# Moving the product of the two gates from GpSimd to VectorE in a gated-attention and multiplicative-FFN kernel

## The chip, the cores and the metric

The kernel runs on one core of one Trainium2 chip. The core has TensorE for matrix products (in the profile PE, its weight loads PEld), VectorE (DVE), ScalarE (ACT), GpSimd (POOL) and SyncE (SP), which here only issues transfers. Each engine takes its instructions strictly in order; across engines they wait for each other by semaphores. The metric is the time of one execution on the device in microseconds (us), the median of several runs.

## The reference

Two blocks follow each other. The first is a recurrent attention with a decaying state, for 4 batches and 8 heads over 768 steps with head size 48:

```python
for t in range(S):
    state = alpha[:, :, t, :, None] * state + np.einsum('bhd,bhe->bhde', k[:, :, t], v[:, :, t])
    y[:, :, t] = np.einsum('bhd,bhde->bhe', q[:, :, t], state)
```

Its output, reshaped to 3072 tokens of 384 values, is the input x of the second block:

```python
a = x @ w1          # 384 -> 1024
b = x @ w2          # 384 -> 1024
h = a * b @ w3      # 1024 -> 1024
return (h @ w_out).astype(np.float32)   # 1024 -> 384
```

The change touches the elementwise product a * b. The four weight matrices come in 64-bit floating point.

## The kernel before

Tokens are handled in 24 chunks of 128, and for the second block in 8 groups of 384 tokens. The feature dimension of 1024 is cut into 8 tiles of 128, so there are 64 tiles of a * b, each 128 features by 384 tokens in 32-bit floats.

A product of full precision is made from three products of reduced precision (`exact`, lines 352 to 363). Each operand is split into a high part, a low part and a mixed part. `exact` does 2n products into one PSUM bank (L358), ScalarE copies that bank scaled into a tile t (L360), TensorE does n products into a second bank (L362), and VectorE combines bank and t (L363). For a gate n is 3.

`gate(g, f)` (L365) does this twice, for w1 and w2, and so gets two tiles r in SBUF. The tiles r and t come from a pool with two buffers each. Then the two r are multiplied into a tile ab (L374, three buffers), and SyncE stores ab to DRAM (L381); in the program the store of a tile is written behind the product of the next one (`store_ab`).

The program has three parts. In the first, the loop over the 24 chunks does the recurrence (matrix products of 48 and 128 columns, masks on VectorE at L308, decays on VectorE at L247, a small product of the state's decay on GpSimd at L294 to L296), converts w1 and w2 from 64 to 32 bits and splits them, and does the first gates in between, half a gate at a time. x goes through DRAM: it is stored by chunk (L336), loaded by group (L341) and split by ScalarE (L347) and VectorE (L348, L349).

In the second part the remaining gates run one after the other. Between them lies the conversion of w_out and w3: `to_fp32` loads a piece of raw 64-bit words (L171, three buffers), takes it apart on ScalarE (L179, L184) and VectorE (L180, L183), and puts it together on VectorE (L186, L187, L189). L187 is the last to read a raw buffer. When a row block of w3 is converted, `fold` transposes it (L401, L403), multiplies it by w_out (L407) and splits the result on ScalarE (L410) and VectorE (L411, L412): w3 and w_out become a single matrix of 1024 by 384.

In the third part the stored ab tiles are loaded (L418), split (L425 to L427) and multiplied by that matrix, again by `exact`, and the output is stored (L434).

The program is written against a planner. It records the instructions in program order with their dependencies, and then orders those of each engine by program priority and by its own estimates of when each can start and how long it takes. So an engine's order on the chip is not always that of the text; L186, L187 and L189 of one piece, for instance, are written together and often stand apart, with L363 of a gate between. The semaphores are placed by the same planner. Raw loads, loads of x and stores of ab all go through SyncE's one queue.

Of the kernel before, what the change touches and what calls it, by code (L numbers as in the profile page):

```python
# [48 lines left out]
def kernel(  # L49
# [12 lines left out]
    nc = tc.nc  # L62
# [289 lines left out]
    def exact(to, w, x, scale):  # L352

        p1, p2 = (bank()[:, 0:to.shape[1]] for _ in range(2))
        n = len(w[0])
        for part in range(2):
            for i in range(n):
                nc.tensor.matmul(p1, w[part][i], x[part][i], start=(part == i == 0), stop=(part == 1 and i == n - 1))  # L358
        t = gw.tile(list(to.shape), FP32, tag="t", name="t")
        nc.scalar.activation(t, p1, AF.Copy, scale=(1.0 + 1.0 / P) * scale)  # L360
        for i in range(n):
            nc.tensor.matmul(p2, w[2][i], x[2][i], start=(i == 0), stop=(i == n - 1))  # L362
        nc.vector.scalar_tensor_tensor(to, p2, -scale, t, op0=ALU.mult, op1=ALU.add)  # L363

    def gate(g, f):  # L365
        r = []
        x = [[st["x3", g][:, part, kk, :] for kk in range(KM)] for part in range(3)]
        for w, scale in zip(w12, (1.0, P * P)):
            r.append(gw.tile([C, TG], FP32, tag="r", name="r"))
            exact(r[-1], [[w[:, part, kk, ds(f * C, C)] for kk in range(KM)] for part in range(3)], x, scale)  # L370
            if len(r) == 1:
                yield
        ab = abp.tile([C, TG], FP32, tag="ab", name="ab")
        nc.gpsimd.tensor_mul(ab, *r)  # L374
        store_ab()
        st["ab"] = g, f, ab

    def store_ab():
        if "ab" in st:
            g, f, ab = st.pop("ab")  # L380
            nc.sync.dma_start(out=abd[g][:, f, :], in_=ab)  # L381
# [92 lines left out]
    for n in range(N):  # L474
        load_a(n + 5)
        load(n + AHEAD)
        scores(n)
        convert(1)
        run(1)
        store_x(n - 1)  # L480
        advance(n)
        outer(n)
        transposed(n + 1)
        decayed(n + 2)
        logs(n + 4)
        convert(2 if n in (0, 1, 2, 3, 4, 5) else 1)
        run(1)
        decays(n + 3)
        load_ends(n + 2)
        convert(1)  # L490
        attend(n)
        if n + 2 in begin:
            load_x(begin[n + 2])
        if n in begin:
            split_x(begin[n], 0)
            fill.extend(gate(begin[n], f) for f in range(FH))
# [20 lines left out]
    for k, (g, tiles) in enumerate(visits):  # L517
        order.append((max(len(todo) - 4, order[-1][0] + 1 if order else 0), len(todo), g, 1 - k % 2))
        todo += [gate(g, f) for f in tiles]
# [59 lines left out]
```

## Time and profile before

| | |
|---|---|
| median of 3 runs | 527.57 us (527.34 to 528.01) |
| profiled execution, its own time | 531.2 us |
| span of the profiled execution | 529.4 us |
| mean granted TensorE clock | 0.973 of full speed |
| GpSimd at L374 | 64 instructions, 78.1 us busy |
| VectorE at L363 for gates | 128 instructions, 69.0 us busy |

The profile records one execution. "Busy" is the time in which an engine had an instruction under way. A row of the timeline gives the start in us from the beginning of the span, the duration, the engine, the source line, the operation, the tile written and the tile read, the number of instructions put together in the row (x), and in brackets the idle time of that engine before it and what ended it. Rows put together overlap a little at their ends. A row of the waits gives who waited, for whom, the total in us, how often, and the longest. SPq is SyncE's queue of transfers.

### The profile page before, as it was taken

Reading aid. Unit: us, or ns where it says so; the run is one execution under the profiler, and the core shown is the slowest. Engines: PE = TensorE matmul, PEld = TensorE weight load, DVE = VectorE, ACT = ScalarE, POOL = GpSimd, SP = SyncE. Lnnn points to the kernel's source line nnn. Section 1 sums busy time; section 2 is a strip of 40 time slices with the busy share of each in tenths; the row PEclk is TensorE's granted clock in tenths of the full one; section 3 lists DMA queues with packets and bytes.
Section 4 is the critical chain, followed back from the end, with each engine's and each line's share of the span. In section 5 each row is a group of like instructions: output and inputs, shape, how many; then the busy total and the mean of one; then the engine's idle time right before and its main releaser. Section 6 shows DMA issues by size and latency. Waiting matters only on the chain. (4 is left out here: it accounts for less than half of the span.)

```text
span 529.4 us, 9440 instructions
## 1 busy us (share of the span) xinstructions
PE 493.5 (93%) x3568; PEld 438.7 (83%) x3568; DVE 366.0 (69%) x546; ACT 245.1 (46%) x443; POOL 96.3 (18%) x105
## 2 busy tenths in 40 slices
PE   3889599999999999998898499999999999999997
PEld 1667478888888888998786388888899999999996
DVE  2699987975545645999999578854365347676771
ACT  3567656564545544545445244433353233343330
POOL 1032012121201121223221422221224310000000
PEclk9979989999999999999899879999999999999999
DMA  9999999889986632555555432220184126555621
GB/s 161 241 187 191 226 213 206 207 170 204 207 201 121 195 117 82 163 173 170 183 176 184 139 110 90 70 91 30 47 226 147 67 79 184 166 165 169 180 79 45
DMA packets 167805, 80.25 MB, mean 152 GB/s; under 512 B 112696, under 2 KB 163152, under 8 KB 167760
## 3 DMA queue, kind: packets, MB, share of 16 engines
q1 hardware_dynamic: 158240, 79.58, 58.3%
q10 hardware_dynamic: 9520, 0.07, 1.1%
q8 instruction: 28, 0.46, 0.4%
q14 instruction: 17, 0.14, 0.1%
HBM read 57.58 MB, written 22.06 MB: 150 GB/s over the span
## 5 line engine op out<-in xcount | busy, mean ns | idle before, releaser
L358 PE MATMUL bank<-x,w 128*128 128x384 f32 x768 | 164.8, 349 | 8.6 <-ACT x L347 5.3
L358 PEld LDWEIGHTS bank<-x,w 128*128 128x128 f32 x768 | 135.5, 191 | 15.0 <-ACT x L347 5.4
L360 ACT ACTIVATE t<-bank 128x384 f32<-128x384 f32 x152 | 73.6, 490 | 122.4 <-PE bank L358 104.1
L374 POOL TENSOR_TENSOR ab<-r 128x384 f32<-128x384 f32 x64 | 78.1, 1221 | 220.7 <-DVE r L363 201.7
L363 DVE SCALAR_TENSOR_TENSOR r<-bank,t 128x384 f32<-128x384 f32 x128 | 69.0, 551 | 62.7 <-ACT t L360 35.9
L362 PE MATMUL bank<-x,w 128*128 128x384 f32 x384 | 90.0, 343 | 9.9 <-ACT t L360 8.5
L362 PEld LDWEIGHTS bank<-x,w 128*128 128x128 f32 x384 | 69.6, 192 | 12.1 <-ACT t L360 9.1
L358 PE MATMUL bank<-w3o,ab 128*128 128x384 f32 x384 | 70.4, 334 | 0.0
L358 PEld LDWEIGHTS bank<-w3o,ab 128*128 128x128 f32 x384 | 66.9, 188 | 0.0
L407 PE MATMUL bank<-wo,w3T 128*128 128x384 f32 x128 | 43.6, 494 | 0.0
L179 ACT ACTIVATE rest<-raw 128x512 f32<-128x512 uint32 (+1 forms) x36 | 23.4, 649 | 33.3 <-DMA raw<-in_moe_w_dram 23.9
L184 ACT ACTIVATE power<-power,rebias 128x512 uint32<-128x512 uint32 (+1 forms) x36 | 25.0, 700 | 27.7 <-DVE power L183 27.5
L407 PEld LDWEIGHTS bank<-wo,w3T 128*128 128x128 f32 x128 | 24.8, 194 | 15.4 <-issue 0.9
L308 DVE TENSOR_TENSOR ms<-bank,keep 128x512 int32<-128x512 int32 x48 | 31.2, 682 | 9.1 <-PE bank L305 8.9
L426 DVE TENSOR_TENSOR ab<-abl,ab 128x1024 fp32r<-128x1024 f32 x24 | 30.1, 1253 | 10.4 <-ACT ab L425 10.4
L362 PE MATMUL bank<-w3o,ab 128*128 128x384 f32 x192 | 37.2, 334 | 0.0
L247 DVE TENSOR_TENSOR qk<-kq,e 128x768 f32<-128x768 f32 x24 | 23.0, 958 | 17.7 <-ACT e L239 16.7
L267 ACT COPY qkT<-bank 128x512 f32<-128x512 f32 x48 | 26.1, 588 | 19.2 <-PE bank L266 19.1
L425 ACT ACTIVATE ab<-abl 128x1024 fp32r<-128x1024 f32 x24 | 25.5, 1062 | 19.2 <-PE bank L362 18.8
L362 PEld LDWEIGHTS bank<-w3o,ab 128*128 128x128 f32 x192 | 33.6, 188 | 0.0
L363 DVE SCALAR_TENSOR_TENSOR o<-bank,t 128x384 f32<-128x384 f32 x24 | 13.4, 558 | 26.8 <-issue 15.2
L427 DVE SCALAR_TENSOR_TENSOR ab<-ab,abl 128x1024 fp32r<-128x1024 f32 x24 | 29.3, 1219 | 0.0
(59 smaller groups left out, 568.1 us busy)
## 6 DMA issues: line engine op xcount, KB each, us to landing
raw<-in_moe_w_dram SPq DMA_DIRECT2D x28, 512.0 KB, 5.3
abd<-ab SPq DMA_DIRECT2D x64, 192.0 KB, 2.2
abl<-abd SPq DMA_DIRECT2D x24, 512.0 KB, 5.4
xT<-xd SPq DMA_DIRECT2D x14, 576.0 KB, 3.9
ac<-in_alpha_dram SPq DMA_DIRECT2D x24, 192.0 KB, 4.4
kq<-in_k_dram SPq DMA_DIRECT2D x24, 192.0 KB, 5.3
kq<-in_q_dram SPq DMA_DIRECT2D x24, 192.0 KB, 4.1
v<-in_v_dram SPq DMA_DIRECT2D x24, 192.0 KB, 4.9
```

The costliest lines, as they stand in the source:

```text
L184: nc.scalar.activation(power, power, AF.Relu, scale=2.0 ** 23, bias=rebias)
L267: nc.scalar.copy(qkT[:, i], tp.rearrange("p (j c) -> p j c", j=NP))
L308: nc.vector.tensor_tensor(ms[:, i].bitcast(I32), sc[i].bitcast(I32), keep_bc, op=ALU.bitwise_and)
L358: nc.tensor.matmul(p1, w[part][i], x[part][i], start=(part == i == 0), stop=(part == 1 and i == n - 1))
L360: nc.scalar.activation(t, p1, AF.Copy, scale=(1.0 + 1.0 / P) * scale)
L362: nc.tensor.matmul(p2, w[2][i], x[2][i], start=(i == 0), stop=(i == n - 1))
L363: nc.vector.scalar_tensor_tensor(to, p2, -scale, t, op0=ALU.mult, op1=ALU.add)
L374: nc.gpsimd.tensor_mul(ab, *r)
L407: nc.tensor.matmul(po, w3T[:, j, :], wo[:, j, :], start=(j == 0), stop=(j == KF - 1))
L425: nc.scalar.activation(t[:, 0], ab, AF.Copy, scale=1.0 - 2.0 ** -13)
L426: nc.vector.tensor_sub(t[:, 1], ab, t[:, 0].bitcast(FP32))
L427: nc.vector.scalar_tensor_tensor(t[:, 2], t[:, 0].bitcast(FP32), 1.0 + 1.0 / P, ab, op0=ALU.mult, op1=ALU.subtract)
```

## The change

The instruction that multiplies the two gate tiles is issued to VectorE instead of GpSimd. Operands, buffers, the store and all loops stay as they were.

```diff
--- before.py
+++ after.py
@@ -371,7 +371,7 @@
             if len(r) == 1:
                 yield
         ab = abp.tile([C, TG], FP32, tag="ab", name="ab")
-        nc.gpsimd.tensor_mul(ab, *r)
+        nc.vector.tensor_mul(ab, *r)
         store_ab()
         st["ab"] = g, f, ab
```

## The prediction

> **What bounds the kernel now.** I read the page's engine shares first, then busy time by stretch, then who made TensorE wait, then the timeline around its longest gap.
>
> ```profile
> span 529.4 us, 9440 instructions
> PE 493.5 (93%) x3568; PEld 438.7 (83%) x3568; DVE 366.0 (69%) x546; ACT 245.1 (46%) x443; POOL 96.3 (18%) x105
> ```
>
> TensorE (PE) is the engine of the span, so a gain can only come out of its idle time or its slow clock. The stretches (columns: length, busy us and count per engine, clock, DMA share, GB/s) say where that lies:
>
> ```profile
> 229.00:262.00 33.00, 29.26 (x154) 27.62 (x153) 33.00 (x50) 16.05 (x30) 11.48 (x10) 0.95 0.61 187
> 262.00:297.00 35.00, 32.93 (x167) 27.61 (x166) 33.98 (x55) 17.74 (x32) 11.51 (x7) 1.00 0.44 142
> 297.00:314.00 17.00, 9.99 (x29) 7.49 (x29) 9.95 (x17) 6.31 (x12) 2.65 (x2) 0.70 0.54 172
> 314.00:426.00 112.00, 112.00 (x593) 101.08 (x592) 63.52 (x96) 43.45 (x80) 29.12 (x25) 1.00 0.31 96
> ```
>
> From 229 to 297 VectorE (DVE) is busy 66.98 of 68 us and TensorE is not: there VectorE sets the pace, with the weight conversion, the splits and the gates all on it. From 297 to 314 nearly everything stands still; from 314 on TensorE has no gap. What TensorE waited for between 229 and 300:
>
> ```profile
> PE bank L358 <- DVE r L363: 2.8, 3, 1.8
> PE bank L362 <- DVE w3o L412: 1.0, 1, 1.0
> PE bank L362 <- ACT t L360: 0.9, 1, 0.9
> PE bank L358 <- ACT t L360: 0.5, 1, 0.5
> ```
>
> That is 5.2 us of short waits. The long gap comes after them, in the timeline:
>
> ```profile
> 290.77 0.54 DVE L363 SCALAR_TENSOR_TENSOR r<-bank,t 128x384 f32<-128x384 f32 x1
> 291.24 0.67 DVE L187 SCALAR_TENSOR_TENSOR power<-raw,power 128x512 uint32<-128x512 uint32 x1
> 291.45 5.41 POOL L374 TENSOR_TENSOR ab<-r 128x384 f32<-128x384 f32 x1 [3.82 <-DVE r L363]
> ...
> 296.89 0.33 SPq L381 DMA_DIRECT2D abd<-ab  x1
> 297.38 0.33 SPq L171 DMA_DIRECT2D raw<-in_moe_w_dram  x1
> ...
> 302.54 0.66 ACT L179 ACTIVATE rest<-raw 128x512 f32<-128x512 uint32 x1 [9.71 <-DMA raw<-in_moe_w_dram]
> ...
> 304.01 1.33 PE L362 MATMUL bank<-x,w 128*128 128x384 f32 x3 [7.53 <-ACT t L360]
> 305.14 2.12 PE L358 MATMUL bank<-x,w 128*128 128x384 f32 x6
> ...
> 308.02 6.31 PE L407 MATMUL bank<-wo,w3T 128*128 128x384 f32 x16
> ```
>
> One product took 5.41 us on GpSimd. Its store (L381) stood at the head of SP's queue until 296.89, the raw weight load (L171) stood behind the store, and ScalarE stood at L179 for that load with L360, whose result TensorE needed, behind it. TensorE idled 7.53 us and then ran slowly.
>
> Why a product that mostly takes 1.0 us took 5.41, and what products do to VectorE, is seen where the two engines meet:
>
> ```profile
> L374 POOL TENSOR_TENSOR ab<-r x64: 992/1019/5412, 75.3 to 426.5; 128x384 f32<-128x384 f32 x64
> 253.88 1.33 POOL L374 TENSOR_TENSOR ab<-r 128x384 f32<-128x384 f32 x1 [2.82 <-DVE r L363]
> 254.26 2.16 DVE L348 TENSOR_TENSOR x<-xT,x 128x1152 fp32r<-128x1152 f32 x1
> ```
>
> L348 starts under the running product and ends 2.16 us later; it lasts until shortly after GpSimd has finished. Groups of VectorE instructions between 215 and 297 (count, then busy us and mean ns) show the same on other lines; the two last rows give the undisturbed duration (the last: minimum/median/maximum, smaller and larger shape):
>
> ```profile
> L186 DVE SCALAR_TENSOR_TENSOR mant<-mant,rest 128x512 f32<-128x512 uint32 x11 | 9.7, 885 | 0.1
> L187 DVE SCALAR_TENSOR_TENSOR power<-raw,power 128x384 uint32<-128x384 uint32 x5 | 5.2, 1040 | 0.0
> L183 DVE TENSOR_SCALAR power<-raw 128x512 uint32<-128x512 uint32 x10 | 6.6, 658 | 0.0
> L180 DVE TENSOR_SCALAR mant<-raw 128x512 uint32<-128x512 uint32 x11 | 6.2, 563 | 0.0
> L183 DVE TENSOR_SCALAR power<-raw 128x384 uint32<-128x384 uint32 x4 | 3.0, 761 | 0.0
> L180 DVE TENSOR_SCALAR mant<-raw 128x384 uint32<-128x384 uint32 x4 | 3.0, 757 | 0.0
> L187 DVE SCALAR_TENSOR_TENSOR power<-raw,power 128x512 uint32<-128x512 uint32 x10 | 6.8, 678 | 0.0
> L180 DVE TENSOR_SCALAR mant<-raw x36: 345/416/1237, 18.8 to 337.7; 128x512 uint32<-128x512 uint32 x28, 128x384 uint32<-128x384 uint32 x8
> ```
>
> A disturbed L180 takes 1.24 where 0.42 is normal: 0.82 us lost. The excess of the six rows is 11 x 0.207 + 5 x 0.495 + 10 x 0.242 + 11 x 0.147 + 4 x 0.416 + 4 x 0.412 = 12.1 us, that is 15 meetings (the plain 128x384 two-input operation takes 0.545, shown below). L348 above is one more; I count 18 meetings for the stretch's 19 products, 14.5 us. So the two engines exclude each other: VectorE loses 0.8 us to nearly every product, and where VectorE runs such operations back to back from 291.24 on, GpSimd is the one that stands.
>
> **The change, part by part.** *Removed:* 64 products on GpSimd, with what they cost VectorE and SP. *Added:* 64 products on VectorE, on the same 128x384 f32 operands in SBUF. Nothing else changes in the text of the kernel; the store stays on SP and waits for VectorE instead. The price:
>
> ```profile
> L189 DVE TENSOR_TENSOR wo<-mant,power x8: 541/545/562, 211.1 to 243.6; 128x384 f32<-128x384 f32 x8
> 257.61 1.01 DVE L363 SCALAR_TENSOR_TENSOR r<-bank,t 128x384 f32<-128x384 f32 x2
> 96.16 0.68 DVE L187 SCALAR_TENSOR_TENSOR power<-raw,power 128x512 uint32<-128x512 uint32 x1
> 96.87 0.69 DVE L189 TENSOR_TENSOR mant<-mant,power 128x512 f32<-128x512 f32 x1
> ```
>
> L189 is the same operation on the same shape: 0.545 us. Two 0.55 us operations in a row take 1.01, so a following operation starts 0.46 after the first. But L189, which reads what L187 just made, starts only 0.71 after it, past its whole 0.68. The product reads the second r straight after it is written, so it costs 0.46 plus the lost overlap of 0.09 and 0.03 of start: 0.58 us. The lower bound, 0.46, holds if the order puts something between. Added between 215 and 297: 19 x 0.58 = 11.0 us, with no cover, since VectorE is full there; the other 45 (26 us) fall where it has idle time, 63.52 busy of 112 after 314 for instance; were that cover gone they would cost their 26 us. The product adds no wait on r (same engine, in order). It must still find its ab buffer stored; there are three, so the store two tiles back must hang for that to bind, and I put it at nothing. SP's queue keeps its order of store and loads, and what is moved past on GpSimd is only the small products of the recurrent state, which then meet no gate product.
>
> Step 1, VectorE's pace, 215 to 297: 14.5 - 11.0 = 3.5 us less VectorE work, which TensorE's short waits (5.2 us) can give back. Bounds 0 (the waits sit elsewhere) and 5.2.
>
> In the Trainium skill, "VectorE: DVE Perf Modes", section "The DRAIN you can't avoid", the next operation does not start until the pipe has emptied; by it every product would cost 0.62, not 0.58, and step 1 would be 2.8. The 1.01 us row contradicts it for independent operations, so I stay at 0.58.
>
> Step 2, the late load: the second r ends at 291.31, the product at about 291.9. L187, which frees the raw buffer, moves behind it and ends near 292.5. The store goes out at 291.9, the load at 292.5 instead of 297.38: 4.9 us earlier, and with the same landing time ScalarE and TensorE resume 4.9 us earlier. The gap shrinks from 7.53 to 2.6. Bounds: 0 (something else holds the load) and 7.5.
>
> Step 3, the clock. Undisturbed rows against those after gaps:
>
> ```profile
> 243.26 1.31 PE L358 MATMUL bank<-x,w 128*128 128x384 f32 x6 [1.76 <-DVE r L363]
> 258.21 1.82 PE L358 MATMUL bank<-x,w 128*128 128x384 f32 x6 [0.87 <-DVE r L363]
> 264.06 0.68 PE L362 MATMUL bank<-x,w 128*128 128x384 f32 x3
> 268.59 5.32 PE L407 MATMUL bank<-wo,w3T 128*128 128x384 f32 x16
> ```
>
> After the 7.53 us gap 1.33, 2.12 and 6.31 stand for 0.68, 1.31 and 5.32: 2.45 us. The clock of 0.95 over 33 us costs 1.65 more. A gap of 1.76 brought no slow row, shorter ones near 258 did, so whether 2.6 us does is open: I take half of both, 2.0 us, bounds 0 and 4.1.
>
> The Trainium skill ("TensorE: Matmul & The Clock Gate", "What's actually happening") has the clock halved after an idle window of about 3.4 us; by it a 2.6 us gap would keep full clock and step 3 would be nearer 4. The 258.21 row, slow after gaps under 1 us, does not follow it.
>
> Sum: 3.5 + 4.9 + 2.0 = 10.4. The profiled execution took 531.2 (1.8 us around its span), 3.6 above the median of 527.57; 531.2 - 10.4 = 520.8, and the same off the median gives 517.2. All idle and clock loss gone would be 5.2 + 7.5 + 4.1 = 16.8: 510.8.
>
> **Rivals.** *Half of it.* The load is early but another wait takes its place, or VectorE stays as full because the order shifts: only step 1, or half of step 2. Gain 2.5 to 6, about 523. For it: ScalarE and SP run in order, and with both engines near full in 229 to 297 small delays add up.
>
> *Slower: the product stuck in VectorE's queue.*
>
> ```profile
> DVE w3o L411 <- ACT w3o L410: 19.6, 6, 6.2
> SPq L381 <- POOL ab L374: 165.1, 52, 8.8
> ```
>
> On GpSimd a product waits for its r alone. On VectorE it waits for all ahead of it, and L411 has stood up to 6.2 us. If the planner, which orders each engine's instructions by its own costs, puts products behind such waits, the store, the load behind it, L179 and TensorE follow as at 291 to 304: 7.5 + 2.45 = 10 us a place. One place eats the gain, a second decides: 517.2 + 20 = 537. Against it: the product is ready the moment r is, and most VectorE waits lie after 314, where the loads have slack.
>
> *No change.* The 5.41 us product belongs to the profiled execution alone and VectorE's relief is used up by other waits: 527.6. Against it: the 0.8 us losses are everywhere in the stretch.
>
> **How the numbers follow.** Likeliest (its own range 512 to 521.5): 0.60. Half: 0.22. Slower: 0.10. No change: 0.08. A measurement tells 0.2% (1.05 us) from nothing, so faster (below 526.5) is 0.82, same 0.08, slower 0.10. The range runs from just under the bound of 510.8 to 526.5, leaving out the last two cases.
>
> **What would show it.** Right: no instruction of GpSimd at L374; L374 on VectorE at about 0.55; L180, L183 and L186 at 0.42, 0.42 and 0.68 with maxima near these; no store waiting 5 us on SP before 300; the gap before L362 near 304 at 3 us or less; the clock of that stretch above 0.9. Wrong: VectorE's busy time between 215 and 297 not falling, a new TensorE gap over 3 us behind ScalarE's L179, or products standing long after their r.

## The result and the profile after

The changed kernel takes 514.56 us (median; 512.42 to 515.54) against 527.79 before, 13.2 us less between the medians; the ratio over all runs is 0.9726 with a 95% interval of 0.9664 to 0.9787, that is 2.7% faster. The forecast was 517.2, its range 510.0 to 526.5. The executions of the kernel before spread over 525 to 534 us, some near 527 and most near 532, which the last experiment looks into. Its profiled execution, at 531.2, is one of the long ones, so the two traces lie further apart (15.6 us of span) than the medians.

The engine shares of the page after:

```profile
span 513.8 us, 9439 instructions
PE 488.9 (95%) x3568; PEld 436.8 (85%) x3568; DVE 373.0 (73%) x610; ACT 246.0 (48%) x443; POOL 17.9 (3%) x41
```

64 products on VectorE raised its busy time by only 7.0 us, because what they cost is nearly paid by what it no longer loses. The stretches of the trace after, columns as before:

```profile
229.00:262.00 33.00, 31.61 (x184) 31.34 (x184) 32.42 (x65) 19.36 (x36) 0.00 (x0) 1.00 0.66 196
262.00:297.00 35.00, 35.00 (x172) 29.16 (x172) 33.09 (x63) 19.77 (x35) 0.00 (x0) 1.00 0.55 173
297.00:314.00 17.00, 17.00 (x85) 14.24 (x84) 16.89 (x32) 8.98 (x17) 0.00 (x0) 1.00 0.61 185
314.00:410.00 96.00, 96.00 (x512) 87.32 (x511) 61.85 (x105) 37.78 (x70) 0.00 (x0) 1.00 0.32 99
```

VectorE is nearly as full as before, but TensorE does not wait for it, and the clock is 1.00 throughout. All that TensorE waited for from the end of the attention part to its last fold is in one row of its waits:

```profile
PE bank L401 <- DVE w L189: 1.4, 1, 1.4
```

Since the stages shift, a stretch bounded by instructions compares better than one bounded by times: from TensorE's last L323 (the end of the attention part) to its last L407 (the last fold). What follows, the rest of the gates and the third part, takes 140.4 us in both traces, up to TensorE's last instruction. The two halves of the stretch, which meet at TensorE's first L401, the start of the first fold, are summed here (length, then busy us of each engine), first before, then after:

```profile
sum 174.10, PE 161.28 PEld 140.90 DVE 136.26 ACT 77.68 POOL 43.47; mean PE 80.64 PEld 70.45 DVE 68.13 ACT 38.84 POOL 21.74
```

```profile
sum 156.36, PE 154.97 PEld 137.42 DVE 131.95 ACT 78.80 POOL 0.00; mean PE 77.49 PEld 68.71 DVE 65.97 ACT 39.40 POOL 0.00
```

The stretch is 17.7 us shorter. VectorE's work in it fell by 4.3 us although it took on the products; its idle time, 174.10 - 136.26 = 37.8 before, is 24.4 after. The attention part gave 1.9 us of the gain back (it ended at 213.02 instead of 211.07 us), which lies within its spread: 211.1 to 215.8 in all traces of this study that keep the first part's start.

Single instructions on VectorE (minimum/median/maximum): L183 before, then three lines after, the product and two of the lines that had met products:

```profile
L183 DVE TENSOR_SCALAR power<-raw x36: 344/415/1240, 19.1 to 338.5; 128x512 uint32<-128x512 uint32 x28, 128x384 uint32<-128x384 uint32 x8
```

```profile
L374 DVE TENSOR_TENSOR ab<-r x64: 546/557/559, 78.2 to 410.6; 128x384 f32<-128x384 f32 x64
L183 DVE TENSOR_SCALAR power<-raw x36: 344/419/430, 19.4 to 322.8; 128x512 uint32<-128x512 uint32 x28, 128x384 uint32<-128x384 uint32 x8
L186 DVE SCALAR_TENSOR_TENSOR mant<-mant,rest x36: 546/683/994, 21.4 to 324.7; 128x512 f32<-128x512 uint32 x28, 128x384 f32<-128x384 uint32 x8
```

The maximum of L183 fell from 1240 to 430 ns. The 994 of L186 lies in the attention part, where the small products of the state are still on GpSimd.

### The profile page after: what moved, and what is told of

The parts are those of the page before. It is cut to its first block, busy times and chain, and to the rows that moved or that the text cites. A ratio compares the mean times of both kernels' runs of the same rounds, so it can differ in the third digit from the quotient of the medians.

```text
span 513.8 us, 9439 instructions
## 1 busy us (share of the span) xinstructions
PE 488.9 (95%) x3568; PEld 436.8 (85%) x3568; DVE 373.0 (73%) x610; ACT 246.0 (48%) x443; POOL 17.9 (3%) x41
## 4 chain that ended last, share of the span: by engine, by line
PE 91%; DVE 3%; DMA 3%; ACT 1%; issue 1%; SPq 0%; ACTq 0%; DVEq 0%
PE bank L358 40%; PE bank L362 20%; PE bank L407 8%; PE bank L305 4%; PE bank L266 4%; PE bank L323 4%; PE bank L319 4%; PE bank L235 3%; PE bank L277 2%; PE bank L401 1%; DMA xT<-xd 1%; DMA ac<-in_alpha_dram 1%; DMA dec<-ends 1%; DVE power L187 1%; DVE ms L308 0%
## 5 line engine op out<-in xcount | busy, mean ns | idle before, releaser
L358 PE MATMUL bank<-x,w 128*128 128x384 f32 x768 | 162.2, 345 | 6.2 <-ACT x L347 6.1
L358 PEld LDWEIGHTS bank<-x,w 128*128 128x128 f32 x768 | 133.8, 189 | 11.1 <-ACT x L347 6.3
L360 ACT ACTIVATE t<-bank 128x384 f32<-128x384 f32 x152 | 74.1, 491 | 129.0 <-PE bank L358 115.5
L363 DVE SCALAR_TENSOR_TENSOR r<-bank,t 128x384 f32<-128x384 f32 x128 | 69.7, 553 | 53.2 <-ACT t L360 44.1
L362 PE MATMUL bank<-x,w 128*128 128x384 f32 x384 | 88.0, 336 | 0.0
L362 PEld LDWEIGHTS bank<-x,w 128*128 128x128 f32 x384 | 68.7, 189 | 0.8 <-PE bank L358 0.5
L407 PE MATMUL bank<-wo,w3T 128*128 128x384 f32 x128 | 42.6, 486 | 0.0
L407 PEld LDWEIGHTS bank<-wo,w3T 128*128 128x128 f32 x128 | 24.1, 190 | 14.9
L374 DVE TENSOR_TENSOR ab<-r 128x384 f32<-128x384 f32 x64 | 35.5, 554 | 1.1
L363 DVE SCALAR_TENSOR_TENSOR o<-bank,t 128x384 f32<-128x384 f32 x24 | 13.4, 558 | 26.6 <-issue 15.6
L247 DVE TENSOR_TENSOR qk<-kq,e 128x768 f32<-128x768 f32 x24 | 22.9, 953 | 13.5 <-ACT e L239 13.2
L179 ACT ACTIVATE rest<-raw 128x512 f32<-128x512 uint32 (+1 forms) x36 | 23.4, 651 | 15.9 <-DMA raw<-in_moe_w_dram 9.1
```

The costliest lines, as they stand in the source:

```text
L374: nc.vector.tensor_mul(ab, *r)
L407: nc.tensor.matmul(po, w3T[:, j, :], wo[:, j, :], start=(j == 0), stop=(j == KF - 1))
```

## The experiments

The theory to test had two parts: VectorE and GpSimd exclude each other, which slows VectorE by 0.8 us a product (step 1), and a starved product holds SP's queue and with it a raw load (steps 2 and 3). The rivals: the planner's new order alone, or the product's shorter way to SP. Ratios are to the kernel before as it ran in the same batch; its median was 531.53 us up to the run with one product moved and 530.69 us after that.

**Exclusion put back in part, order kept.** GpSimd multiplies each finished product by itself into an unused tile. In its trace the order of instructions on TensorE, VectorE and SyncE is that of the changed kernel.

```diff
-        ab = abp.tile([C, TG], FP32, tag="ab", name="ab")
+        ab, twin = (abp.tile([C, TG], FP32, tag=x, name=x, bufs=n) for x, n in (("ab", 3), ("twin", 1)))
...
         nc.vector.tensor_mul(ab, *r)
+        nc.gpsimd.tensor_mul(twin, ab, ab)
```

> The product stays on VectorE; GpSimd multiplies each finished product tile by itself into a tile that nobody reads. The outputs are computed as before. The order on TensorE, VectorE, ScalarE and SyncE is that of the changed kernel. Theory (the two engines exclude each other, about 0.8 us of VectorE for each meeting): VectorE pays 0.46 to 0.58 for its own product and 0.8 for the twin, 12 to 15 us more in a stretch that is full, so the gain is lost: 525 to 540 us, L180, L183, L186 and L187 again with maxima of 1.2 to 1.5 us. Rival (the gain comes from the new order, or from the product reaching SyncE's queue sooner): nothing waits for the twin, so 512 to 516 us.

524.18 us, ratio 0.9909 (0.9869 to 0.9949): 9.6 us of the 13.2 are lost again, just short of the range expected. The sum of the stretch in this run:

```profile
sum 163.68, PE 158.11 PEld 138.68 DVE 140.66 ACT 78.13 POOL 38.13; mean PE 79.05 PEld 69.34 DVE 70.33 ACT 39.06 POOL 19.07
```

Two groups of its instructions, by line:

```profile
L186 DVE SCALAR_TENSOR_TENSOR mant<-mant,rest x36: 546/680/1305, 21.6 to 334.8; 128x512 f32<-128x512 uint32 x28, 128x384 f32<-128x384 uint32 x8
L374 POOL TENSOR_TENSOR twin<-ab x64: 825/942/1939, 79.9 to 421.5; 128x384 f32<-128x384 f32 x64
```

The maxima of L186 and L187 come back as expected (1.31 and 1.32 us); those of L180 and L183 reach only 1.05. Nobody reads the twin, so its cost is exclusion: 7.3 us in the stretch (163.68 - 156.36), with VectorE 8.7 us busier. A rival without exclusion has no way to explain this. But the twins put back only a part of the exclusion, because they meet other instructions than the products did (L349, which no product had lengthened, has a median of 1.98 us here instead of 1.35). Measured against the median of the same line and shape in the changed kernel, VectorE's instructions in the stretch last 9.2 us too long here; in the kernel before it was 21.0 us, 0.6 us for each of its 34 products there. The stretch is still 10.4 us shorter than before, although VectorE is 4.4 us busier than it was then: the amount of VectorE's work is not all that counts.

**Only one part of the products moved.**

```diff
-        nc.vector.tensor_mul(ab, *r)
+        (nc.vector if "late" in st else nc.gpsimd).tensor_mul(ab, *r)
...
     part1.close()
+    st["late"] = True
```

> Only the products traced after the first part go to VectorE; those of the first part, where the attention chunks run, stay on GpSimd. Theory: TensorE had no idle time to give back before 215 us, so all of the gain is here: 512 to 517 us. Rival (the first part's products delay the weight conversion or the loads that the second part then lacks): only part of the gain, 518 to 525 us.

514.29 us, 0.971 (0.9659 to 0.9762): the whole gain, as the theory expected. The reverse, with the two engines exchanged in that line:

> The reverse: only the products of the first part go to VectorE. Theory: 526 to 529 us, as before, with one product of 4 us or more on GpSimd and a TensorE gap behind it still there near 290 to 304. Rival (the first part matters): 518 to 524 us.

531.05 us, 0.9966 (0.9917 to 1.0015): nothing that can be told from no change. Both expected ranges were missed; the theory's 526 to 529 lay around the 527.57 of the first runs, while the kernel before had a median of 531.53 in this batch. The starved product is still there, as the group of the products left on GpSimd shows:

```profile
L374 POOL TENSOR_TENSOR ab<-r x47: 992/1070/5411, 216.6 to 427.4; 128x384 f32<-128x384 f32 x47
```

So the 17 products of the attention part are worth nothing either way: from 75 us, where the first product starts, to 211 us TensorE has no gap over 0.4 us to give back.

**One product moved.**

```diff
-        nc.gpsimd.tensor_mul(ab, *r)
+        st["count"] = st.get("count", 0) + 1
+        (nc.vector if st["count"] == 36 else nc.gpsimd).tensor_mul(ab, *r)
```

> Only the 36th product, the one that took 5.41 us on GpSimd, goes to VectorE; the other 63 stay. Theory of the late load (steps 2 and 3 of the prediction, 7.5 us of gap and 2.45 us of slow clock): most of the gain comes from this one product, 517 to 521 us. Rival (VectorE's pace is what counts, and with the other 63 on GpSimd the next product is starved or the next load late instead): 525 to 528 us.

526.75 us, 0.9931 (0.9899 to 0.9963): 4.8 us below the median of the kernel before in this batch (531.53). The expectation of 517 to 521 failed; the time is in the rival's range. The sum of the stretch in its trace:

```profile
sum 167.00, PE 159.38 PEld 138.39 DVE 135.48 ACT 77.10 POOL 38.99; mean PE 79.69 PEld 69.20 DVE 67.74 ACT 38.55 POOL 19.50
```

Its timeline of TensorE at the end of what had been the long gap (start, length, instruction, and in brackets the wait before it):

```profile
301.03 0.79 PE L362 MATMUL bank<-x,w 128*128 128x384 f32 x3 [1.56 <-ACT t L360]
301.70 1.31 PE L358 MATMUL bank<-x,w 128*128 128x384 f32 x6
```

The long gap is 1.56 instead of 7.53 us and nothing runs slowly behind it. The stretch is 7.1 us shorter than in the profiled execution of the kernel before; 10.6 us remain to the changed kernel.

**The store taken out of SP's queue.** The product stays on GpSimd, which issues its store too.

```diff
-            nc.sync.dma_start(out=abd[g][:, f, :], in_=ab)
+            nc.gpsimd.dma_start(out=abd[g][:, f, :], in_=ab)
```

> The product stays on GpSimd, and GpSimd issues its store too, so that SyncE's queue and the raw loads in it no longer wait for a product. Theory of the late load as in the prediction (a store that waits for its product holds the raw load): the long gap near 296 to 304 falls to 3 us or less, the exclusion stays, 523 to 528 us. Rival (SyncE's queue waiting for GpSimd products is most of the difference between the two kernels): 514 to 518 us.

526.33 us, 0.9925 (0.9889 to 0.996), as the theory expected. The sum of the stretch in its trace:

```profile
sum 165.94, PE 158.44 PEld 136.88 DVE 135.86 ACT 77.12 POOL 65.87; mean PE 79.22 PEld 68.44 DVE 67.93 ACT 38.56 POOL 32.94
```

Its timeline, the starved product on GpSimd and the end of the gap that had been the long one on TensorE:

```profile
293.30 5.46 POOL L374 TENSOR_TENSOR ab<-r 128x384 f32<-128x384 f32 x1 [2.90 <-DVE r L363]
299.51 0.79 PE L362 MATMUL bank<-x,w 128*128 128x384 f32 x3 [1.18 <-ACT t L360]
```

The product is starved as before, 5.46 us, behind the same VectorE lines, and TensorE hardly notices: 1.18 us. The planner also moved some other VectorE and ScalarE instructions here, but together with the single-product run, which moves hardly any, this shows the path of the long gap: product, store, raw load. It also shows that SP's queue is not the rest of the gain.

**The product twice on VectorE.**

```diff
-        ab = abp.tile([C, TG], FP32, tag="ab", name="ab")
+        ab, twin = (abp.tile([C, TG], FP32, tag=x, name=x, bufs=n) for x, n in (("ab", 3), ("twin", 1)))
         nc.vector.tensor_mul(ab, *r)
+        nc.vector.tensor_mul(twin, *r)
```

> As changed, and VectorE multiplies the same pair a second time into a tile that nobody reads. Nothing else is left out. Theory (VectorE still sets the pace from 215 to 314 us, where it was busy 96 of 99 us after the change): about 25 extra products of 0.47 to 0.58 us there without cover, 12 to 14 us: 522 to 528 us, with TensorE idle again in that stretch. Rival (TensorE sets the pace, VectorE's fullness is work done ahead of need): 514 to 517 us.

524.36 us, 0.987 (0.9795 to 0.9945), inside the theory's range. The sum of the stretch in this run:

```profile
sum 164.22, PE 157.98 PEld 139.77 DVE 147.11 ACT 78.82 POOL 0.00; mean PE 78.99 PEld 69.89 DVE 73.56 ACT 39.41 POOL 0.00
```

TensorE's longest gap in it, from the timeline:

```profile
267.90 1.09 PE L401 MATMUL bank<-ident,w 128*128 128x128 f32 x4 [4.01 <-DVE w L189]
```

VectorE is 15.2 us busier and the stretch 7.9 us longer: about half of what is added shows. In the twin run above 8.7 us more gave 7.3. The planner moved other VectorE instructions in this run too, so the size is less sure than in the twin run. Both say that after the change VectorE stands close behind TensorE and has little to spare.

**A GpSimd instruction that only writes.** One of the two r tiles is filled with zeros after each product, before it is written anew.

```diff
         nc.vector.tensor_mul(ab, *r)
+        nc.gpsimd.memset(r[0], 0.0)
```

> As changed, and GpSimd fills one of the two gate tiles with zeros behind each product; the tile is not read again before it is written anew. So GpSimd has one instruction per product again, on the same size, which only writes SBUF. Theory (the exclusion is with GpSimd instructions that read SBUF; on two-input VectorE instructions a fill has no effect): 514 to 518 us, L186, L187 and L348 at their undisturbed durations, at most L180 and L183 longer. Rival (any GpSimd instruction on SBUF stops VectorE): as with the twin, 521 to 526 us.

515.27 us, 0.97 (0.9637 to 0.9762), as the changed kernel. The group of the fills in this run:

```profile
L374 POOL MEMSET r<- x64: 413/418/1587, 78.5 to 411.5; 128x384 f32 x64
```

One place of its timeline where a fill meets the conversion:

```profile
313.37 0.41 DVE L180 TENSOR_SCALAR mant<-raw 128x512 uint32<-128x512 uint32 x1
313.56 1.59 POOL L374 MEMSET r<- 128x384 f32 x1 [4.12 <-DVE ab L374]
...
314.38 0.42 DVE L183 TENSOR_SCALAR power<-raw 128x512 uint32<-128x512 uint32 x1
314.71 0.68 DVE L186 SCALAR_TENSOR_TENSOR mant<-mant,rest 128x512 f32<-128x512 uint32 x1
315.31 0.68 DVE L187 SCALAR_TENSOR_TENSOR power<-raw,power 128x512 uint32<-128x512 uint32 x1
```

The fill takes 0.42 us alone and 1.59 here: it stood while four L180 and L183 ran in a row and was done 0.44 us after L186 began, during L186, which kept its 0.68. So a fill excludes the one-input L180 and L183 and not the two-input L186, while a product, which reads SBUF, had excluded both. In the Trainium skill, "SBUF — State Buffer", section "Who interferes with whom", a VectorE instruction with two inputs in SBUF contends with a GpSimd instruction that reads SBUF and not with one that only writes, and one in the fast two-port mode contends with either. These rows agree with the first; they agree with the second if L180 and L183 run in that mode, which no trace here shows.

**The first gates one chunk later.**

```diff
-    begin = {6 + 4 * g: g for g in range(5)}
+    begin = {7 + 4 * g: g for g in range(5)}
```

> As changed, with the first gates begun one chunk later (7 + 4g instead of 6 + 4g). After the change nearly all of TensorE's idle time lies before the first gate, 6.1 us of it waiting for the first x tile at 62 to 68 us. Theory: chunk work fills that wait, 509 to 513 us. Rival (the chunk work there waits for its own input loads, and the gates put off come back later): 514 to 518 us.

521.95 us, 0.983 (0.9767 to 0.9893): slower than the changed kernel, and outside both expected ranges. The timeline of TensorE in this run, where the chunk work now stands ahead of the first gate:

```profile
65.64 1.65 PE L235 MATMUL bank<-la,after 128*128 128x384 f32 x2 [2.80 <-ACT la L227]
...
76.39 1.33 PE L358 MATMUL bank<-x,w 128*128 128x384 f32 x3 [3.74 <-ACT x L347]
```

The wait of 6.1 us became two, 2.80 for the chunk's input and 3.74 for the x tile, and the first gate began 8 us later. The attention part ended as in the changed kernel (212.84 us); the stretch up to the last fold is 1.8 us longer, and what follows it 3.1 us. So the gates put off came back later, as the rival said, and cost more than it expected.

**The kernel before, unchanged, in four more executions.**

> The kernel before, unchanged, profiled once more. Its times lie in two groups, 525 to 529 us and 531 to 534 us. If the late load comes in some executions only: an execution of 530 us or more has a product of 5 us and a TensorE gap of over 6 us behind it, one of 525 to 529 us has neither a gap over 3 us after 215 us. If the late load is always there: the gap is in it whatever its time.

> The same kernel as the look before, once more, with the same expectation: the long gap goes with the time of 530 us or more, or it is always there.

> The kernel before once more, to meet an execution of 525 to 529 us: if the long gap is not always there, such an execution lacks it; one of 530 us or more has it again.

> As the look before it: an execution of 525 to 529 us without the long gap, or one of 530 us or more with it.

Times: 533.6, 531.43, 527.89 and 534.24 us. The first, second and fourth have a product of 5.41 to 5.42 us on GpSimd and a TensorE gap of 7.14, 7.25 and 7.54 us behind it. The third has neither in that size: its longest gap after 215 us is 2.98 us, just under the 3 us expected of a short execution. The third's sum of the stretch:

```profile
sum 169.04, PE 159.62 PEld 138.42 DVE 136.37 ACT 77.05 POOL 40.65; mean PE 79.81 PEld 69.21 DVE 68.19 ACT 38.52 POOL 20.32
```

Its timeline at the same place as in the prediction, and the gap:

```profile
293.11 0.69 DVE L187 SCALAR_TENSOR_TENSOR power<-raw,power 128x512 uint32<-128x512 uint32 x1
293.32 1.34 POOL L374 TENSOR_TENSOR ab<-r 128x384 f32<-128x384 f32 x1 [3.92 <-DVE r L363]
293.71 1.51 DVE L186 SCALAR_TENSOR_TENSOR mant<-mant,rest 128x512 f32<-128x512 uint32 x1
...
301.42 0.88 PE L362 MATMUL bank<-x,w 128*128 128x384 f32 x3 [2.98 <-ACT t L360]
302.10 2.28 PE L358 MATMUL bank<-x,w 128*128 128x384 f32 x6
```

Here GpSimd got through and L186 stood, 1.51 for 0.68 us. In the long executions L186 went first and the product stood. So the starved product comes in some executions and not in others, and the five executions put its price in the stretch at 4 to 5 us (173.0 to 174.1 against 169.0). The single-product run is another 2.0 us shorter in the stretch. It is 3.5 us shorter behind the first fold (113.57 against 117.10 us), where the gap of 2.98 and the slow rows after it remain even in the short execution, and 1.5 us longer ahead of it.

The times of all executions fit this: not one of the twenty executions of the single-product run and of the run with the store moved took more than 527.9 us, while of the 47 of the kernel before 28 took more than 530.

## Why the prediction was right, and where it was not

*What bounds the kernel* held. All of the gain lies after the attention part, where TensorE had gaps (moving the late products gives all, the early ones nothing).

*Step 2 and step 3 together*, 4.9 + 2.0 = 6.9 us, against 7.1 us in the stretch when only that product was moved. So close an agreement is partly luck: 0.8 of the 2.0 stood for the slow clock from 229 to 262 us, and the single-product run did not get that back (53.43 us ahead of the first fold against 53.51). The chain of product, store, raw load, L179 and L360 is supported by the run that takes the store out of it. A gap of 2.6 was forecast to remain; 1.56 and 1.18 remain in the two runs that free the load, and in the changed kernel there is none. On the clock, half of 4.1 us was taken. The clock is 1.00 in all four stretches after, and TensorE's busy time in the stretch fell by 6.3 us (161.28 to 154.97), so at least all of it came back. But the 2.98 us gap was followed by 2.28 for 1.31 us, at a granted clock of 0.50 from 302.0 to 304.3 us, so the caution about 2.6 us was justified. The Trainium skill ("TensorE: Matmul & The Clock Gate", "What's actually happening") names an idle window of about 3.4 us, by which so short a gap should have kept full clock; this row does not follow it, as the 258.21 one did not.

What the prediction did not see is that this event is not in every execution. It was in four of the five profiled executions of the kernel before, and the rival "no change" had that half right. The forecast took its loss off a median of 527.57 that came from three executions near 527, while the later comparisons had 531.53 and 530.69. If those three lacked the starved product, as the one profiled at 527.89 did, most of steps 2 and 3 was taken off a time that did not hold it. From its own profiled execution the prediction had 520.8, and the profiled execution after took 515.5, a gain of 15.7 us where 10.4 were added up. The steps were too small and the time they were taken off was low; the two errors cancel in part. That 517.2 lies only 2.6 us from the measured median is partly luck.

*Step 1*, 3.5 us, is the term that was mis-sized. Its own quantity was right: the 14.5 us that VectorE was held up from 215 to 297 are confirmed by the durations after the change, and VectorE's work in the stretch fell by 4.3 us. (Its row of L348 says it more sharply than the prediction did: L348 ended 1.2 us after the product, so it ran nearly all of its 1.35 us behind it.) But from the single-product run to the changed kernel, where the late load no longer counts, the stretch fell by 10.6 us with 3.5 us less VectorE work (135.48 to 131.95). The step took it that TensorE gets back what VectorE's work loses, capped at the 5.2 us of TensorE's short waits. Of the 10.6 us, 6.2 were TensorE's idle time and 4.4 its slower rows (159.38 to 154.97), which step 3 had counted at 0.8 for this part. The two halves of the stretch, ahead of the first fold and from there on, first of the single-product run, then of the changed kernel (columns as before), show more:

```profile
214.07:267.50 53.43, 49.71 (x270) 48.05 (x271) 53.33 (x82) 28.17 (x52) 15.17 (x13) 0.97 0.54 171
267.50:381.07 113.57, 109.67 (x536) 90.35 (x535) 82.15 (x130) 48.94 (x91) 23.82 (x20) 1.00 0.34 112
```

```profile
213.02:259.86 46.84, 46.84 (x270) 46.81 (x271) 45.61 (x88) 26.54 (x49) 0.00 (x0) 1.00 0.59 177
259.86:369.38 109.52, 108.13 (x536) 90.61 (x535) 86.34 (x157) 52.26 (x94) 0.00 (x0) 1.00 0.40 125
```

Ahead of the first fold VectorE was full and TensorE waited; after the change TensorE is full. That is 6.6 of the 10.6 us. VectorE's work there fell by 7.7 us, for two reasons. The exclusion that went (10.7 us) was more than the 14 products that came (6.6 us at 0.47 each). And the planner's new order puts nine conversion instructions of w3 behind the first fold that had run ahead of it: four of L180 and L183 at 0.33 us from start to start and five of L186, L187 and L189 at 0.60, together 4.3 us, while one L363 more came in. With these nine still there and without that L363, VectorE would have had about 49.4 us of work, 2.6 more than TensorE's 46.84. That is an estimate from these counts; by it about 2.6 of the 6.6 us are the order's and the rest is the exclusion's. From the first fold on, the other 4.1 us, order and exclusion were not told apart, nor the product being ready 0.8 us after its second r instead of 1.3 (medians in the stretch): no run here has the one without the others.

The price of the product, 0.58 us, was the upper end: in 27 of the 34 products of the stretch after, the planner put another instruction between the second r and the product, so that the 0.46 of independent operations held. The rule of the Trainium skill that would have made it 0.62 ("VectorE: DVE Perf Modes", "The DRAIN you can't avoid") is further off. The same paragraph of it adds that a next operation that is not held starts earlier, which the prediction left out; the starts in a row, 0.46 to 0.47 us apart for operations of 0.55, agree with that.

*Slower, the product stuck in VectorE's queue*, was not seen: TensorE's only gap after 100 us is 1.39 us long, and it waits for a weight conversion. *Half of it* was not seen either.

Of the signs named, one was badly chosen: "no store waiting 5 us on SP before 300". After the change a store does wait on SP from 292 to 297 us, and the raw loads behind it go out at 297.92, but TensorE has no gap there.

## What to carry to other kernels

When GpSimd and VectorE work on SBUF at the same time, the duration of an instruction in a profile is not its price: compare a line's maximum with its minimum before reckoning what a move costs. Here moving an elementwise product to the fuller engine made room on it, because in the stretch that counts each product had held that engine up by 0.6 us and cost 0.47 as its own. Where the fuller engine sets the pace, look also at what the planner then runs later: by the estimate above about 2.6 us of this gain came from work put off to a place where that engine had idle time. In a queue that runs in order, a store that waits for its producer holds every load behind it, and one late producer can stop an engine that has nothing to do with it.

## What was not expected of the hardware

Which of the two engines stands is decided by little. In the long execution L187 began at 291.24 and the product at 291.45; in the short one 293.11 and 293.32, the same 0.21 us apart. In the first the next VectorE instruction went ahead and the product took 5.41 us, in the second the product went ahead and took 1.34. What decides is not visible in these traces.

A GpSimd fill and a GpSimd product are different neighbours: 64 fills left the time at 515.27 us, 64 products that nobody reads made it 524.18.
